# Three scheduling changes in a fused attention and gMLP kernel on one core: which units are scored by rows, when a modulation weight is used, and when the group loads are issued

## Chip, cores and metric

One core of one Trainium2 chip. The metric is the device time of the whole program in microseconds (us); the profile's span, from the first to the last instruction, is about 1.9 us shorter.

The engines are called as the profile calls them: PE (TensorE, matmuls), ACT (ScalarE), DVE (VectorE), POOL (GpSimd, which also issues DMAs), SP (SyncE, which issues the DMA transposes).

## The reference

Grouped-query attention, modulated by a condition vector `c`, followed by a gated MLP. Sizes: 2048 queries and keys, model width 512, 32 query heads in 8 groups, head width 128, MLP width 1792.

```python
mod = silu(c) @ w_mod                       # six rows of 512: sa, ca, ga, sb, cb, gb
h = layernorm(x) * (1 + ca) + sa
q = (h @ wq)                                # 32 heads of 128
p = softmax(q k^T / sqrt(128));  o = p v    # 4 heads share one group's k, v
x = x + ga * (o @ wo)
h = layernorm(x) * (1 + cb) + sb
z = gelu(h @ w_in); z1, z2 = halves of z; z2 = layernorm(z2)
x = x + gb * ((z1 * (w_sp @ z2 + b_sp)) @ w_out)
```

## The kernel before

The attention is a software pipeline over 128 *units*, a unit being one group (8) times 128 queries (16). Iteration `it` computes the scores of unit `it` in eight slots, and in the same slots the PV product of an earlier unit, the output projection of a still earlier one, and a piece of the next q. A unit's scores are made in one of two ways:

```python
    TURN_A, TURN_B = 3 * CT, (HKV - 1) * NT          # 12, 112
    def by_rows(u):
        return TURN_A <= u < TURN_B and u % 2 == 0
    def pv_at(u):
        return u + 3 if by_rows(u) else u + 1
```

- *Not by rows*: keys on the partitions. The exponentials land as PV needs them; PV is 64 matmuls of 129 columns (the last one sums the row), then DVE normalises and SP issues one small transpose, `oT<-onorm`.
- *By rows*: queries on the partitions. ACT accumulates the row sums, DVE normalises 128x2048 for each of four heads, and SP issues four transposes of 128x2048 into `pT`. PV is then 16 matmuls of 512 columns, two units later than otherwise, because the transposes need time.

The four buffers for a row unit's exponentials are slices of tiles that are idle during attention: three in the tile of `w_in`, one in `wmod_a`. Head 3's buffer is read by a transpose that the program places in slot 1 of the *next* unit, and it is needed again two units after its own.

```python
def turn_rows(u, hh):                       # DVE, then SP
    ...
    nc.vector.tensor_scalar(out=pn[hh], in0=pn[hh], scalar1=rinv, ...)
    nc.sync.dma_start_transpose(out=pTs[u][:, :, hh * P : (hh + 1) * P], in_=pn[hh])

def mod_rows():                             # ga and gb as rows on all partitions
    ...                                     # 32 one-column matmuls, two copies into modc
    for part, rows in ((2, ga_rows), (5, gb_rows)):
        line = dram.tile([D], FP32, ...)
        nc.gpsimd.dma_start(out=line[:].rearrange("(dt p) -> p dt", p=P), in_=modc[:, cols])
        nc.gpsimd.dma_start(out=rows[:], in_=line[:].partition_broadcast(P))
```

`mod_rows` therefore makes a chain of four DMAs on POOL: 2 KB out to DRAM, read back to all partitions, and once more. `at(it, slot, fn)` places a piece of work in *program order*. On PE and ACT, which are kept busy, that is also its time. On POOL, which has little to do, an instruction runs as soon as its buffer is free and the one before it is done, often many units earlier.

```python
    at(9, 4, mod_cols_b); at(10, 4, mod_rows)
    for g in range(1, HKV):
        it = (g - 1) * NT
        at(it + 7, 6, load_k(g))            # SP, a transpose out of DRAM
        at(it + 8, 3, load_v(g)); at(it + 9, 3, load_wo(g)); at(it + 7, 3, load_wq(g))   # POOL
```

## Time and profile before

| | before |
|---|---|
| device time, first three runs | 1316.68 us median, 1314.65 to 1318.89 |
| span of the profiled run | 1314.1 us |
| busy PE / ACT / DVE | 1305.1 / 1105.0 / 657.4 us |
| mean DMA rate | 119 GB/s, 156.79 MB |
| a pair of units, one by rows | 17.44 us |
| a pair of units, none by rows | 17.62 us |
| waits of PE in the waits view | 3.0 us |

The durations of a unit, here and below, are the distances between every eighth exponential of ACT in the timeline: unit *u* begins with exponential 8*u*. The waits view lists engine, line and tile, what it waited for, the total, the number and the longest.

### The profile page before, as it was taken

How to read it: one execution, taken by the hardware profiler on the slowest of the kernel's cores; microseconds unless marked ns; L12 is line 12 of the kernel's file. 1: busy time of each engine (PE TensorE's matmuls, PEld its weight loads, DVE VectorE, ACT ScalarE, POOL GpSimd, SP SyncE). 2: the span in 40 equal slices, each digit the busy share in tenths (PEclk: the TensorE clock that was granted, in tenths of full speed). 3: DMA queues.
4: the chain of work that ended last, by engine and by line, in shares of the span. 5: the costliest groups of instructions: out<-in, count | busy, mean ns of one | idle time of the engine just before them, and what ended most of it. 6: DMA issues, size and time to landing. Idle time of an engine off the chain costs nothing.

```text
span 1314.1 us, 25092 instructions
## 1 busy us (share of the span) xinstructions
PE 1305.1 (99%) x9959; PEld 755.5 (57%) x9959; DVE 657.4 (50%) x1612; ACT 1105.0 (84%) x1461; POOL 52.0 (4%) x96
## 2 busy tenths in 40 slices
PE   9999999999999999999999999999999999999998
PEld 5666555555555555555555555555556666644445
DVE  6624445444454544444455544444452566784444
ACT  7899999999999999999999999999998899650000
POOL 1101000000000000000000000000000000120000
PEclk9999999999999999999999999999999999999999
DMA  7554988878988888988897877688762232143200
GB/s 181 123 67 58 180 161 141 140 125 158 153 144 138 144 141 138 135 142 157 153 143 129 155 141 144 124 166 151 140 126 76 45 62 48 29 117 80 69 21 27
DMA packets 537741, 156.79 MB, mean 119 GB/s; under 512 B 527280, under 2 KB 533680, under 8 KB 537616
## 3 DMA queue, kind: packets, MB, share of 16 engines
q1 hardware_dynamic: 530592, 135.97, 60.3%
q0 software_dynamic: 4432, 16.91, 4.6%
q10 hardware_dynamic: 2592, 2.23, 0.5%
q8 instruction: 80, 1.31, 0.4%
q14 instruction: 45, 0.37, 0.1%
HBM read 21.89 MB, written 2.10 MB: 18 GB/s over the span
## 4 chain that ended last, share of the span: by engine, by line
PE 98%; DMA 1%; DVE 0%; issue 0%; ACT 0%; ACTq 0%; DVEq 0%
PE o_ps L1069 21%; PE s_ps L1013 20%; PE o_ps L1048 13%; PE s_ps L994 13%; PE misc L1101 8%; PE misc L944 8%; PE misc L1426 7%; PE s_ps L1260 2%; PE s_ps L1299 2%; PE o_ps L1447 1%; DMA pT<-wmod_a 1%; PE o_ps L785 1%; PE s_ps L1447 1%; PE misc L854 0%; PE o_ps L944 0%; DVE hT L813 0%
## 5 line engine op out<-in xcount | busy, mean ns | idle before, releaser
L1020 ACT ACTIVATE wsp<-s_ps 128x1024 bf16<-128x1024 f32 x408 | 416.2, 1025 | 19.5 <-PE s_ps L1013 3.5
L1013 PE MATMUL s_ps<-qT,kT 128*128 128x512 bf16 x1248 | 370.9, 379 | 1.9 <-ACT wmod_a L1001 1.6
L1001 ACT ACTIVATE win_sb<-s_ps 128x1024 bf16<-128x1024 f32 x300 | 307.0, 1025 | 6.2 <-ACT win_sb L1001 0.8
L1069 PEld LDWEIGHTS <-wsp 128*128 128x128 bf16 x3264 | 218.5, 98 | 96.3
L1069 PE MATMUL o_ps<-v,wsp 128*128 128x129 bf16 x3264 | 251.6, 220 | 0.0
L994 PE MATMUL s_ps<-kT,qT 128*128 128x512 bf16 x800 | 237.9, 379 | 0.0
L1048 PE MATMUL o_ps<-pT,v 128*128 128x512 bf16 x800 | 237.3, 379 | 0.0
L1020 ACT ACTIVATE pT<-s_ps 128x1024 bf16<-128x1024 f32 x216 | 217.3, 1026 | 20.6 <-PE s_ps L1013 8.3
L1101 PE MATMUL misc<-wo_g,oT 128*128 128x512 bf16 x512 | 194.0, 379 | 0.0
L1013 PEld LDWEIGHTS <-kT 128*128 128x128 bf16 x1248 | 121.0, 98 | 117.0 <-issue 4.4
L944 PE MATMUL misc<-hT,wq_g 128*128 128x512 bf16 (+2 forms) x520 | 187.0, 371 | 0.1
L1069 PEld LDWEIGHTS <-pT 128*128 128x128 bf16 x1728 | 115.3, 98 | 49.6
L955 DVE CAST qT<-misc 128x512 bf16<-128x512 f32 x125 | 85.5, 684 | 112.2 <-PE misc L944 112.2
L1048 PEld LDWEIGHTS <-v 128*128 128x128 bf16 x800 | 78.2, 98 | 94.4
L1069 PE MATMUL o_ps<-v,pT 128*128 128x129 bf16 x1728 | 132.5, 220 | 0.0
L1057 DVE CAST oT<-o_ps 128x512 bf16<-128x512 f32 x50 | 34.6, 691 | 173.7 <-PE o_ps L1048 173.7
L1035 DVE TENSOR_SCALAR win_sb<-win_sb,rall 128x2048 bf16<-128x2048 bf16 x150 | 113.0, 753 | 5.7 <-DVE rall L1034 0.5
L994 PEld LDWEIGHTS <-qT 128*128 128x128 bf16 x800 | 78.2, 98 | 52.5 <-issue 0.2
L1001 ACT ACTIVATE wmod_a<-s_ps 128x1024 bf16<-128x1024 f32 x100 | 102.4, 1024 | 2.3 <-DMA pT<-wmod_a 2.3
L1426 PE MATMUL misc<-wsp,z 128*128 128x512 bf16 (+2 forms) x560 | 100.7, 336 | 0.0
L1080 DVE RECIPROCAL rall<-o_ps 128x2 f32<-128x2 f32 x156 | 26.6, 170 | 135.1 <-PE o_ps L1069 131.4
L1031 DVE TENSOR_TENSOR tot<-rs 128x1 f32<-128x1 f32 x200 | 30.7, 154 | 120.6 <-ACT win_sb L1001 119.1
(106 smaller groups left out, 856.5 us busy)
## 6 DMA issues: line engine op xcount, KB each, us to landing
wq_g<-in_A_wq_dram POOLq DMA_DIRECT2D x7, 512.0 KB, 5.5
v<-in_A_v_cache_dram POOLq DMA_DIRECT2D x7, 512.0 KB, 5.9
wo_g<-in_A_wo_dram POOLq DMA_DIRECT2D x7, 512.0 KB, 3.8
pT<-win_sb SPq DMA_TRANSPOSE x150, 4.9
wsp<-in_w_mod_dram POOLq DMA_DIRECT2D x1, 2048.0 KB, 10.4
out_dram<-yout ACTq DMA_DIRECT2D x16, 128.0 KB, 1.7
win_sb<-in_B_w_in_dram POOLq DMA_DIRECT2D x1, 1792.0 KB, 9.3
x_sb<-in_A_x_dram SPq DMA_DIRECT2D x3, 512.0 KB, 5.3
```

The lines of the kernel that those rows point to most:

```text
L944: nc.tensor.matmul(ps[0][:, o0 : o0 + n], lhsT=wqs[g][:, dt, hh * DH : (hh + 1) * DH], rhs=hTs[ch][:, dt, c0 : c0 + n], start=(dt == 0), s ...
L955: nc.vector.tensor_copy(out=dst, in_=src)
L994: nc.tensor.matmul(s_ps[:, c * 512 : (c + 1) * 512], lhsT=qTs[b][:, hh, jj * P : (jj + 1) * P], rhs=groups[g]["kT"][:, k0 : k0 + 512], sta ...
L1001: nc.scalar.activation(out=pn[hh][:, half * HK : (half + 1) * HK], in_=s_ps[:], func=ACT.Exp, scale=inv_sqrt_dh, accum_out=rsums[u][:, i : ...
L1013: nc.tensor.matmul(s_ps[:, h * 512 : (h + 1) * 512].rearrange("p (r q) -> p r q", r=REP), lhsT=groups[g]["kT"][:, kt * P : (kt + 1) * P], ...
L1020: nc.scalar.activation(out=pTs[u][:, 2 * i : 2 * i + 2, :], in_=s_ps[:].rearrange("p (k q) -> p k q", k=2), func=ACT.Exp, scale=inv_sqrt_dh,)
L1035: nc.vector.tensor_scalar(out=pn[hh], in0=pn[hh], scalar1=rinv, scalar2=None, op0=ALU.mult)
L1048: nc.tensor.matmul(o_pss[u][:], lhsT=groups[g]["v1"][:, kt, 0:DH], rhs=pTs[u][:, kt, :], start=(kt == 0), stop=(kt == NKT - 1),)
L1057: nc.vector.tensor_copy(out=oTs[u][:], in_=o_pss[u][:].rearrange("p (r q) -> p r q", r=REP))
L1069: nc.tensor.matmul(o_ps[:, hh % 2, 0 : DH + 1], lhsT=pTs[u][:, kt, hh * P : (hh + 1) * P], rhs=groups[g]["v1"][:, kt, 0 : DH + 1], start=( ...
L1101: nc.tensor.matmul(X_ps[:], lhsT=oTs[u][:, hh, :], rhs=groups[g]["wo"][:, hh, :], start=(hh == 0), stop=(hh == REP - 1),)
L1426: nc.tensor.matmul(g_ps[:, :n], lhsT=z2[:, st, f * P : (f + 1) * P], rhs=wsp[t][:, st, c0 : c0 + n], start=(st == 0), stop=(st == NT - 1 a ...
```

## The change

The intent is to take more of PE's work in the cheaper, wide form: by rows from unit 8 on and not 12, and three units (112, 116, 120) of the last group too. For that the `wsp` buffer and the weights in it must be free earlier (the second part of `w_mod` is used in iterations 4 and 5, not 9 and 10), PV of the late row units comes five units later so that each fills an iteration that would have none, and the group loads are spread, one per pair of units.

```diff
-    TURN_A, TURN_B = 3 * CT, (HKV - 1) * NT
+    TURN_A, TURN_B = 2 * CT, (HKV - 1) * NT
     def by_rows(u):
-        return TURN_A <= u < TURN_B and u % 2 == 0
+        return u % 2 == 0 if TURN_A <= u < TURN_B else u % 4 == 0 and TURN_B <= u < NU - CT
     def pv_at(u):
-        return u + 3 if by_rows(u) else u + 1
+        return u + 1 if not by_rows(u) else u + 3 if u < TURN_B else u + 5
+    # three buffers (pT0, pT1, wsp), each unit takes the one that is free first
...
-    at(TURN_B + 3, 5, lambda: nc.gpsimd.dma_start(out=win_sb, in_=win_dram))
-    at(9, 4, mod_cols_b)
-    at(10, 4, mod_rows)
+    at(NU - CT - 1, 2, lambda: nc.gpsimd.dma_start(out=win_sb, in_=win_dram))
+    at(4, 4, mod_cols_b)
+    at(5, 4, mod_rows)
...
-    at(TURN_B + 4, 0, wsp0)
+    at(NU + 1, 0, wsp0)                      # and its 16 loads with it
...
-        at(it + 7, 6, lambda g=g: load_k(g))
-        at(it + 8, 3, lambda g=g: load_v(g))
-        at(it + 9, 3, lambda g=g: load_wo(g, nc.gpsimd))
-        at(it + 7, 3, lambda g=g: load_wq(g, nc.gpsimd))
+        at(it + 7, 4, lambda g=g: load_wq(g, nc.gpsimd))
+        at(it + 9, 5, lambda g=g: load_k(g))
+        at(it + 11, 4, lambda g=g: load_v(g))
+        at(it + 13, 4, lambda g=g: load_wo(g, nc.gpsimd))
```

More of the change, by code (lines that the diff above doesn't have):

```diff
@@ L962 @@
     NU = HKV * NT
-    TURN_A, TURN_B = 3 * CT, (HKV - 1) * NT
+    TURN_A, TURN_B = 2 * CT, (HKV - 1) * NT
     def by_rows(u):
-        return TURN_A <= u < TURN_B and u % 2 == 0
+        return u % 2 == 0 if TURN_A <= u < TURN_B else u % 4 == 0 and TURN_B <= u < NU - CT
     def pv_at(u):
-        return u + 3 if by_rows(u) else u + 1
+        return u + 1 if not by_rows(u) else u + 3 if u < TURN_B else u + 5
+    users, homes = dict(pT0=-2, pT1=-1, wsp=CT + 2), {}
+    for u in range(NU):
+        homes[u] = min(users, key=lambda k: users[k])
+        assert users[homes[u]] < u
+        users[homes[u]] = pv_at(u)
     rsums, pTs, onorms, oTs, xaccs, o_pss, h2Ts = {}, {}, {}, {}, {}, {}, {}
@@ L982, in qk @@
         if i == 0:
-            if TURN_A <= u <= TURN_B + 1 and u % 2 == 1:
+            if homes[u] == "wsp":
                 pTs[u] = wspp.tile([P, NT, 512], BF16, name="wsp")
             else:
-                pTs[u] = late.tile([P, NKT, 512], BF16, name="pT")
+                pTs[u] = late.tile([P, NKT, 512], BF16, name=homes[u], bufs=1)
             if by_rows(u):
@@ L1230, in set_fill @@
             if hole:
-                it, slot = hole, k // 2
+                it, slot = divmod(hole * NSLOT + k // 2 - 1, NSLOT)
             if b == 1:
@@ L1239, in wsp0 @@
         wsp[0] = wspp.tile([P, NT, 512], BF16, name="wsp")
-    at(TURN_B + 4, 0, wsp0)
+    at(NU + 1, 0, wsp0)
     for st in range(NT):
-        at(TURN_B + 4 + st // 2, 2 + 4 * (st % 2), lambda st=st: load_wsp(wsp[0], 0, st))
+        at(NU + 1 + st // 4, 2 * (st % 4), lambda st=st: load_wsp(wsp[0], 0, st))
     for g in range(1, HKV):
         it = (g - 1) * NT
-        at(it + 7, 6, lambda g=g: load_k(g))
-        at(it + 8, 3, lambda g=g: load_v(g))
-        at(it + 9, 3, lambda g=g: load_wo(g, nc.gpsimd))
-        at(it + 7, 3, lambda g=g: load_wq(g, nc.gpsimd))
+        at(it + 7, 4, lambda g=g: load_wq(g, nc.gpsimd))
+        at(it + 9, 5, lambda g=g: load_k(g))
+        at(it + 11, 4, lambda g=g: load_v(g))
+        at(it + 13, 4, lambda g=g: load_wo(g, nc.gpsimd))
     zs = {}
@@ L1350 @@
             zs["z2"] = z2p.tile([P, NT, FH], BF16, name="z2")
-        pvs = [u for u in (it - 3, it - 1) if 0 <= u < NU and pv_at(u) == it]
-        wos = [u for u in (it - 5, it - 3) if 0 <= u < NU and pv_at(u) + 2 == it]
+        pvs = [u for u in (it - 5, it - 3, it - 1) if 0 <= u < NU and pv_at(u) == it]
+        wos = [u for u in (it - 7, it - 5, it - 3) if 0 <= u < NU and pv_at(u) + 2 == it]
         wf = [fn for u in wos for fn in wo_proj(u)]
```

## The prediction

> **What bounds the kernel now.** I read the page first: busy time, the 40 slices and the chain that ended last.
>
> ```profile
> PE 1305.1 (99%) x9959; PEld 755.5 (57%) x9959; DVE 657.4 (50%) x1612; ACT 1105.0 (84%) x1461; POOL 52.0 (4%) x96
> ...
> PEclk9999999999999999999999999999999999999999
> ...
> PE 98%; DMA 1%; DVE 0%; issue 0%; ACT 0%; ACTq 0%; DVEq 0%
> ```
>
> TensorE (PE) works in 99% of the span at full clock, and the chain is 98% PE. So a change gains only what it takes off PE, or what it takes out of a stall of PE. The waits view then says how much of the second kind there is: of PE 3.0 us in all (three waits), but a stalled matmul counts as running, so I looked at ScalarE (ACT) too, whose exponentials free the score banks.
>
> The program has 128 units (a group of keys times 128 queries), each with eight exponentials of 128x1024, so every eighth exponential of ACT starts a unit. In every one of the 128 iterations PE does a unit's scores (16 matmuls of 512 columns), the PV product of an earlier unit, up to four matmuls of the output projection and up to four of the next q. Fifty units (even ones, 12 to 110) are "by rows": scores with queries on the partitions, transposed by DMA, PV as 16 matmuls of 512 columns at L1048. The other 78 do PV as 64 matmuls of 129 columns at L1069. The timeline of PE shows one slot (an eighth of an iteration) of either kind, first with the narrow PV, then with the wide one:
>
> ```profile
> 202.50 0.59 PE L994 MATMUL s_ps<-kT,qT 128*128 128x512 bf16 x2
> 202.93 0.62 PE L1069 MATMUL o_ps<-v,wsp 128*128 128x129 bf16 x8
> 203.39 0.38 PE L944 MATMUL misc<-hT,wq_g 128*128 128x512 bf16 x1
> 203.60 0.59 PE L994 MATMUL s_ps<-kT,qT 128*128 128x512 bf16 x2
> ...
> 210.21 0.59 PE L1013 MATMUL s_ps<-qT,kT 128*128 128x512 bf16 x2
> 210.64 0.59 PE L1048 MATMUL o_ps<-pT,v 128*128 128x512 bf16 x2
> 211.07 0.38 PE L944 MATMUL misc<-hT,wq_g 128*128 128x512 bf16 x1
> 211.29 0.59 PE L1013 MATMUL s_ps<-qT,kT 128*128 128x512 bf16 x2
> ```
>
> Start to start counts here, not the durations, which overlap. Eight narrow PV matmuls take 203.39 - 202.93 = 0.455 us, two wide ones 211.07 - 210.64 = 0.43 us; the slots last 1.10 and 1.08 us. So an iteration lasts 8 x 1.10 = 8.81 us with a narrow PV and 8 x 1.08 = 8.64 with a wide one. The timeline of ACT agrees: two units with rows between them start
>
> ```profile
> 193.46 8.52 ACT L1020 ACTIVATE wsp<-s_ps 128x1024 bf16<-128x1024 f32 x8
> 210.90 8.52 ACT L1020 ACTIVATE wsp<-s_ps 128x1024 bf16<-128x1024 f32 x8
> ```
>
> 17.44 us apart. In the last group, where no unit is by rows, unit follows unit in 8.81, a pair in 17.62. **A unit by rows is worth 0.18 us**, about 1% of a pair, and no more. (Bare ACT needs less: it makes eight exponentials by rows in 8.0 us where PE is ahead, at 118 to 126 us.)
>
> Last I looked for real stalls. ACT has one of size:
>
> ```profile
> 539.88 0.19 ACT L1001 ACTIVATION_READ_ACCUMULATOR win_sb<-s_ps 128x1 f32 x1
> 542.18 1.02 ACT L1001 ACTIVATE wmod_a<-s_ps 128x1024 bf16<-128x1024 f32 x1 [2.11 <-DMA pT<-wmod_a]
> ...
> DMA to landing us min/median/max: 4.2/4.3/13.3
> ```
>
> The last line is of the transposes out of wmod_a. One of 50 took 13.3 us instead of 4.3; it was issued at 528.82, and a load of wq_g issued at 528.90 took 12.2 us itself, against 4.6 to 4.8 in two other groups. ACT then waited for its buffer, and unit 60 lasted 10.75 us instead of 8.82.
>
> **What the Trainium skill says.** "TensorE: Matmul & The Clock Gate", section "Wait — 56ns, not 53.3ns?", gives start to start at full clock as the columns over 2.4 GHz plus about 2.5 ns: 55.6 ns for 128, 215.7 for 512. The trace agrees: 0.455 us / 8 = 57 ns for 129 columns, 0.43 / 2 = 216 ns for 512. So 64 narrow matmuls are 3.62 us and 16 wide ones 3.46: the wide form saves the fixed cost and the 129th column, nothing else. "DMA: Bandwidth & Descriptors", section "Issuing engines are not separate DMA queues", says that transfers from all issuing engines run on the same 16 DMA engines and interleave; the collision at 528.8 us, where both transfers were slow, agrees.
>
> **The change part by part.**
>
> By rows from 8, and 112, 116, 120: five more units (8 and 10 early, three late), so 55. PE loses 5 x 48 = 240 matmuls and 5 x 0.18 = **0.9 us**. ACT gets 40 accumulator reads, and DMA 20 transposes of 4.3 to 4.4 us less five small ones, all beside PE.
>
> PV five units later in the last group: deferral only. The old order ended its rows with two PVs in iteration 113 (unit 113 lasted 12.20 us = 8.81 plus one PV of about 3.4, nothing lost) and two output projections in iteration 115 (9.99 us against 8.81 plus 4 x 0.216 = 9.67: 0.3 us lost). Now 112 follows at 117, 116 at 121, 120 at 125, each into an iteration without another PV but the last. Two PVs meet in 125 (about 8.0 + 3.46 us) and two projections in 127, where there is no q projection. I count **0.3 us** gained, perhaps 0.
>
> The hole: the first deferred PV leaves an iteration short, at 13 before, at 9 now, filled with the same 16 q projections. Units 12 to 15 took 31.73 us; their PE work is about 30.6 (7.94, 7.78, 7.94, 6.91 from 0.216 and 0.057 us each), as ACT limits two of them. The same loss of about a microsecond moves to 8 to 11. Only the wait of 0.24 us for a transpose at 140 us may go, as the w_mod rows' small DMAs no longer run there: **0.2 us**.
>
> Second part of w_mod early: its 64 one-column matmuls (0.8 us in each of iterations 9 and 10, which lasted 9.61 instead of 8.81) move to 4 and 5, at the same cost. The load is at the same place; it was issued at 37.1 and landed at 47.5 us. Iteration 4 begins at 46.0 (ACT) and its slot 4 is at 50.0, so 2.5 us are to spare. VectorE and GpSimd work moves along, off the path.
>
> Group loads: wq, v and wo keep their order on GpSimd, which runs ahead and waits for a free buffer (wq_g waits 323 us in total), so their times hardly move; only k, on SP's queue, starts two units later. **0.**
>
> win_sb later (unit 123) and spatial weights wsp[0] at iteration 129: win_sb needs 9.3 us and is first read at 1130.7, some 40 us later. The 16 transposes of wsp[0] are issued at about 1.3 us each, 21 us from 1139 on; their use begins at 1184.9. The next 32 loads may start at 1166 instead of 1160, for use from 1209 on. **0.**
>
> Sum: 0.9 + 0.3 + 0.2 = 1.4 us less: 1316.68 - 1.4, rounded to **1315.3 us**.
>
> **The rivals.** (a) *DMA becomes the bound.* The DMA share is 0.8 to 0.9 in the row phase and 0.16 to 0.33 in the last group; four extra transposes every four units fit there, and a row unit at 8 starts only after the hT transposes (landed at 76.4). Against it: in 50 row units one transpose in the waits of ACT cost 2.1 us. It would cost some 2 to 4 us by chance, more if a PV waited for its transposes, which have over a unit to spare. (b) *The tail slips.* SP issues in order, and the xnT transposes of the last tiles now queue among wsp[0]'s loads. VectorE is nearly full there (14.5 of 16 us from 1139 to 1155), and the last z2 normalisation ends at 1183.9, some 4 us before PE reads those tiles. A slip of over 4 us would lengthen the span one for one; I estimate 1 to 2 at most, so hidden. (c) *The early move stalls PE:* wmod_b landing later than iteration 4's slot 4 costs its lateness, 2 to 5 us. Against it: nothing before its load changes. For a gain instead: v and wo of the next group now queue on GpSimd behind the mod rows, so that they no longer share DMA with the hT transposes at 60 to 76 us (8.5 to 13.7 us to landing); but PE did not wait there. (d) *The collisions vanish* with the k load moved: 2 us less. For it only that unit 60 was such a case; against it, that the transfer there was wq_g, whose time stays.
>
> **Range and chances.** The three runs of before spread over 4.2 us, 0.3%, about three times the gain I expect. With the chance stalls of (a) and (d) on either side: 1312.0 to 1318.5. Two per cent is 26 us; no part of the working comes near it. Faster by over 2%: 0.01; within: 0.97; slower: 0.02, for a PE or DMA stall that repeats in each group.
>
> **What would show it.** In the changed trace: 880 wide and 4672 narrow PV matmuls (before 800 and 4992), PE still 98% of the chain, row pairs at 17.44 us, units of the last group at 8.64 where 112 and 116 have their PV, 8.81 elsewhere; no unit of 12.20 at 113 but one near 11.5 at 125; units 4 and 5 longer by 0.8, 9 and 10 not. Wrong would be: PE waiting at L854 for wmod_b, PV waiting for a pT transpose in the last group, a gap before the first spatial matmul, or row pairs of another length. Then the step "DMA fits beside PE" fails, and the time leaves the range upwards.

## The result, and the profile after

| | before | after |
|---|---|---|
| median, same chip | 1315.66 us (4 runs, 1313.84 to 1318.89) | 1315.51 us (4 runs, 1315.24 to 1316.04) |
| ratio after / before | | 0.9997, 95% interval 0.9975 to 1.0018 |
| span of the profiled run | 1314.13 us | 1313.84 us |

A ratio is the mean time of one kernel's fast runs over that of the other's of the same rounds, so not quite the ratio of the medians. The times are the same within the noise, and the predicted 1315.3 us lies 0.2 us off. The two spans, cut at the same units, say that this agreement hides errors that cancel:

| stretch (units) | before | after | difference | predicted |
|---|---|---|---|---|
| start, 0 to 3 | 45.98 | 46.12 | +0.14 | 0 |
| 4 to 15 | 103.79 | 106.16 | **+2.37** | -0.6 |
| 16 to 111 | 838.85 | 837.12 | **-1.73** | 0 |
| 112 to 127 | 142.22 | 141.23 | -0.99 | -0.84 |
| after the last exponential | 183.30 | 183.21 | -0.09 | 0 |

(Predicted: two early row units and the wait at unit 14 make -0.36 - 0.24; three late ones and the pair of projections -0.54 - 0.3.)

First what stayed as it was. The busy times and the chain of the changed kernel, from its page:

```profile
PE 1294.6 (99%) x9545; PEld 744.9 (57%) x9719; DVE 675.8 (51%) x1657; ACT 1109.2 (84%) x1501; POOL 52.9 (4%) x96
...
PE 97%; DMA 1%; issue 1%; DVE 0%; SPq 0%; ACT 0%
```

PE is still 97% of the chain. The weight loads count the matmuls of the two forms better than the matmul records, of which some are missing; from the groups by line and form:

```profile
L1076 PEld LDWEIGHTS <-pT 128*128 128x128 bf16 x4544 | 303.8, 98 | 133.2
L1055 PEld LDWEIGHTS <-v 128*128 128x128 bf16 x880 | 86.1, 98 | 103.8
...
L1076 PEld LDWEIGHTS <-wsp 128*128 128x128 bf16 x128 | 8.6, 98 | 3.3
```

The reader sees 880 wide PV matmuls and 4544 + 128 = 4672 narrow ones, as predicted. The row pairs last 17.44 us, iterations 113, 117 and 121 of the last group 8.57 (their neighbours 8.82 to 8.87), 125 11.40. Units 4 and 5 are longer by 0.8 us each, as predicted.

The -1.73 us is the wait in unit 60 of the kernel before (10.75 us), which this trace of the changed one doesn't have. The +2.37 us is new. It sits in unit 10, which lasts 10.87 us; PE's waits show its first part:

```profile
PE misc L1108 <- DMA oT<-onorm: 1.2, 1, 1.2
PE s_ps L1020 <- ACT wmod_a L1008: 0.9, 1, 0.9
```

Before, the second of these two lines read 1.6 us (in unit 60) and the first did not exist. In the timeline of PE they are these instructions:

```profile
102.90 0.62 PE L1076 MATMUL o_ps<-v,pT 128*128 128x129 bf16 x8
104.69 0.39 PE L1108 MATMUL misc<-wo_g,oT 128*128 128x512 bf16 x1 [1.17 <-DMA oT<-onorm]
...
108.00 0.38 PE L1108 MATMUL misc<-wo_g,oT 128*128 128x512 bf16 x1
109.33 0.59 PE L1020 MATMUL s_ps<-qT,kT 128*128 128x512 bf16 x2 [0.95 <-ACT wmod_a L1008]
```

The output projection of unit 7 waits for its `oT`. That transpose is small and lands 2.6 us after its issue in the median of this trace (2.4 at the least). SP's timeline shows why it was late:

```profile
82.96 1.19 SPq L1096 DMA_TRANSPOSE oT<-onorm  x1
86.28 12.86 SPq L1045 DMA_TRANSPOSE wsp<-win_sb  x3
99.30 1.20 SPq L1096 DMA_TRANSPOSE oT<-onorm  x1
100.60 3.75 SPq L1045 DMA_TRANSPOSE wsp<-wmod_a  x1
104.41 2.86 SPq L743 DMA_TRANSPOSE kT<-in_A_k_cache_dram  x1
```

The second column is the time that SP takes to *issue*, as the profile records it. Three of unit 8's transposes occupied SP for 12.86 us, the first alone for 7.9, and the `oT` of unit 7 stood behind them in the same queue. It was issued at 99.30 and landed at 104.64. What slowed them is in the timeline of POOL:

```profile
60.91 0.83 POOL L1180 DMA_DIRECT2D mod<-modc  x1 [0.85 <-DVE modc L1178]
70.44 0.57 POOL L1181 DMA_DIRECT2D ga_rows<-mod  x1 [8.71 <-DMA mod<-modc]
71.00 0.76 POOL L1180 DMA_DIRECT2D mod<-modc  x1
81.05 0.55 POOL L1181 DMA_DIRECT2D gb_rows<-mod  x1 [9.29 <-DMA mod<-modc]
81.59 0.76 POOL L720 DMA_DIRECT2D wq_g<-in_A_wq_dram  x1
...
82.48 1.17 POOL L728 DMA_DIRECT2D v<-in_A_v_cache_dram  x1
83.63 0.77 POOL L738 DMA_DIRECT2D wo_g<-in_A_wo_dram  x1
```

Before, POOL issued these three loads of group 1 (1.5 MB) at 59 to 61 us:

```profile
59.11 0.82 POOL L720 DMA_DIRECT2D wq_g<-in_A_wq_dram  x1
...
60.11 1.31 POOL L728 DMA_DIRECT2D v<-in_A_v_cache_dram  x1
61.41 0.76 POOL L738 DMA_DIRECT2D wo_g<-in_A_wo_dram  x1
```

Now the chain of `mod_rows` stands ahead of them, each copy to DRAM takes over 9 us, and the loads start at 81.6 to 83.6, just ahead of the first transposes of unit 8 at 86.3. That is the theory for the experiments: **theory 1, the held-up loads meet unit 8's transposes**. Its rivals: the short iterations around the first deferred PV cost this wherever they stand; the load of k, now in SP's queue at 104 us, is to blame; or it is chance, as in unit 60.

### The profile page after: what moved, and what is told of

Its sections match the earlier page's. It is cut to its first block, busy times and chain, and to the rows that moved or that the text cites. A ratio compares the mean times of both kernels' runs of the same rounds, so it can differ in the third digit from the quotient of the medians.

```text
span 1313.8 us, 24616 instructions
## 1 busy us (share of the span) xinstructions
PE 1294.6 (99%) x9545; PEld 744.9 (57%) x9719; DVE 675.8 (51%) x1657; ACT 1109.2 (84%) x1501; POOL 52.9 (4%) x96
## 4 chain that ended last, share of the span: by engine, by line
PE 97%; DMA 1%; issue 1%; DVE 0%; SPq 0%; ACT 0%
PE o_ps L1076 20%; PE s_ps L1020 20%; PE s_ps L1001 15%; PE o_ps L1055 14%; PE misc L1108 8%; PE misc L944 8%; PE misc L1433 7%; PE s_ps L1267 2%; PE s_ps L1306 2%; PE o_ps L1454 1%; PE s_ps L1454 0%; DMA kT<-in_A_k_cache_dram 0%; DMA oT<-onorm 0%; PE o_ps L944 0%; PE misc L854 0%
## 5 line engine op out<-in xcount | busy, mean ns | idle before, releaser
L1027 ACT ACTIVATE pT<-s_ps 128x1024 bf16<-128x1024 f32 x568 | 576.6, 1024 | 34.0 <-PE s_ps L1020 9.5
L1076 PEld LDWEIGHTS <-pT 128*128 128x128 bf16 x4544 | 303.8, 98 | 133.2
L1076 PE MATMUL o_ps<-v,pT 128*128 128x129 bf16 x4544 | 349.8, 220 | 1.2
L1020 PE MATMUL s_ps<-qT,kT 128*128 128x512 bf16 x1168 | 347.4, 379 | 2.8 <-ACT wmod_a L1008 0.9
L1008 ACT ACTIVATE win_sb<-s_ps 128x1024 bf16<-128x1024 f32 x330 | 337.5, 1024 | 7.2 <-PE s_ps L1001 1.2
L1001 PE MATMUL s_ps<-kT,qT 128*128 128x512 bf16 x857 | 257.0, 379 | 2.9
L1055 PE MATMUL o_ps<-wsp,v 128*128 128x512 bf16 x426 | 128.1, 379 | 0.6
L1055 PE MATMUL o_ps<-pT,v 128*128 128x512 bf16 x410 | 123.8, 380 | 0.6
L1433 PEld LDWEIGHTS <-z 128*128 128x128 bf16 x560 | 50.6, 98 | 48.5
L1121 DVE TENSOR_TENSOR xacc<-misc,xacc 128x512 f32<-128x512 f32 x112 | 76.2, 680 | 0.0
```

The costliest lines, as they stand in the source:

```text
L1001: nc.tensor.matmul(s_ps[:, c * 512 : (c + 1) * 512], lhsT=qTs[b][:, hh, jj * P : (jj + 1) * P], rhs=groups[g]["kT"][:, k0 : k0 + 512], sta ...
L1008: nc.scalar.activation(out=pn[hh][:, half * HK : (half + 1) * HK], in_=s_ps[:], func=ACT.Exp, scale=inv_sqrt_dh, accum_out=rsums[u][:, i : ...
L1020: nc.tensor.matmul(s_ps[:, h * 512 : (h + 1) * 512].rearrange("p (r q) -> p r q", r=REP), lhsT=groups[g]["kT"][:, kt * P : (kt + 1) * P], ...
L1027: nc.scalar.activation(out=pTs[u][:, 2 * i : 2 * i + 2, :], in_=s_ps[:].rearrange("p (k q) -> p k q", k=2), func=ACT.Exp, scale=inv_sqrt_dh,)
L1055: nc.tensor.matmul(o_pss[u][:], lhsT=groups[g]["v1"][:, kt, 0:DH], rhs=pTs[u][:, kt, :], start=(kt == 0), stop=(kt == NKT - 1),)
L1076: nc.tensor.matmul(o_ps[:, hh % 2, 0 : DH + 1], lhsT=pTs[u][:, kt, hh * P : (hh + 1) * P], rhs=groups[g]["v1"][:, kt, 0 : DH + 1], start=( ...
```

## The experiments

Twelve kernels ran; all gave correct results. Kernels are compared only within the same rounds. The stretches are from one trace of each, in us. No kernel differs by 2% from the kernel before; the intervals that exclude 1 are those of e1 and e3 (faster) and of e6 and e4 (slower).

| run | median (runs) | before | ratio (95%) | units 4-7 | 8-11 | 12-15 | 16-111 | 112-127 |
|---|---|---|---|---|---|---|---|---|
| changed, again | 1316.74 (6) | 1319.01 (11) | 0.9988 (0.9966, 1.0009) | 36.79 | 34.03 | 34.88 | 837.12 | 141.23 |
| e1 | 1314.20 (6) | 1319.01 | 0.9967 (0.9946, 0.9989) | 38.95 | 31.90 | 34.88 | 837.12 | 141.23 |
| e3 | 1314.01 (6) | 1319.01 | 0.9963 (0.9942, 0.9984) | 36.79 | 35.23 | 31.90 | 838.96 | 141.18 |
| e6 | 1328.17 (6) | 1319.01 | 1.0070 (1.0039, 1.0100) | 36.79 | 43.39 | 34.88 | 837.12 | 141.23 |
| e8 | 1316.84 (6) | 1317.04 (11) | 0.9993 (0.9975, 1.0011) | 36.79 | 31.91 | 34.88 | 841.37 | 141.23 |
| e9 | 1320.09 (6) | 1317.04 | 1.0012 (0.9995, 1.0030) | 36.79 | 31.90 | 34.88 | 844.00 | 141.23 |
| e4 | 1320.91 (4) | 1317.04 | 1.0025 (1.0003, 1.0046) | 36.79 | 35.29 | 35.23 | 845.46 | 137.54 |
| e2 | 1315.67 (4) | 1317.04 | 0.9986 (0.9965, 1.0007) | 36.85 | 35.17 | 31.63 | 837.07 | 142.23 |
| e10 | 1313.84 (5) | 1315.61 (9) | 0.9988 (0.9974, 1.0001) | 36.79 | 31.90 | 34.88 | 837.12 | 141.98 |
| e12 | 1313.77 (5) | 1315.61 | 0.9987 (0.9973, 1.0001) | 35.28 | 36.77 | 31.63 | 837.07 | 142.24 |
| e7 | 1316.38 (1) | | | 36.79 | 34.28 | 34.88 | 837.07 | 142.24 |
| e5 | 1320.91 (1) | | | 36.79 | 34.31 | 34.88 | 838.65 | 145.40 |

**The changed kernel again.** No edit.

> The changed kernel once more, unaltered, for its spread and to see whether the wait in unit 10 belongs to the kernel or to chance. Theory 1 (the loads of group 1, held up on GpSimd behind the w_mod rows, meet the transposes of unit 8): the wait recurs, unit 10 lasts 10.4 to 11.2 us, units 8 to 11 together 34 to 35 us, time 1315.2 to 1316.2 us. Theory 2 (chance, like the wait of the kernel before in unit 60): unit 10 lasts about 8.4 us, units 8 to 11 about 32 us, and the time falls to about 1313.3 us.

Units 8 to 11 took 34.03 us: the wait recurs, so it belongs to the kernel. (34.28 in e7 and 34.31 in e5, which leave this part alone, 34.49 in the first trace.) The times spread over 1315.0 to 1318.6, wider than expected, and the median is 1 us higher than in the first call; the kernel before ran up to 1323.3 here.

**e1: the loads of group 1 ahead of the w_mod rows.**

```diff
+        if g == 1:
+            at(5, 3, lambda: load_wq(1, nc.gpsimd))
+            at(5, 3, lambda: load_v(1))
+            at(5, 3, lambda: load_wo(1, nc.gpsimd))
+            at(it + 9, 5, lambda: load_k(1))
+            continue
```

> The changed kernel with one edit: wq, v and wo of group 1 are issued just ahead of the w_mod rows (iteration 5, slot 3), so that they start at about 60 us and not at 82 to 84. Theory 1 (these loads slow unit 8's transposes, SP's queue holds up the oT transpose of unit 7, and PE waits for it in iteration 10): no wait in unit 10, units 8 to 11 together 31.7 to 32.3 us instead of 34.5, time 2.2 to 2.8 us below the changed kernel, 1312.7 to 1313.3. Rival (the short iterations around the first deferred PV cost this wherever they stand): units 8 to 11 stay at 34 to 35 us and the time at 1315.5. A loss elsewhere is possible: the hT transposes of 61 to 76 us then share DMA with 1.5 MB again.

Units 8 to 11 fell to 31.90 us, so theory 1 holds for unit 10. But most of the gain reappeared in unit 7, 10.77 us instead of 8.75, by the same kind of wait:

```profile
80.70 0.39 PE L1108 MATMUL misc<-wo_g,oT 128*128 128x512 bf16 x1 [1.85 <-DMA oT<-onorm]
```

The loads, the small DMAs and the hT transposes now all ran at 60 to 81 us, and another `oT` took 13.1 us to land. In the trace the net gain over the repeat of the changed kernel is zero (spans 1313.16 and 1313.14); in the timed runs the median fell by 2.5 us, as expected (to 1314.20, not to 1313, as the changed kernel itself was slower), but with no gain in the trace that fall is not explained: it may be chance waits in the runs that left no trace. The prediction of the loss elsewhere was right, its size was not foreseen.

**e3: rows from unit 12 again.**

```diff
-    TURN_A, TURN_B = 2 * CT, (HKV - 1) * NT
+    TURN_A, TURN_B = 3 * CT, (HKV - 1) * NT
```

> The changed kernel with rows from unit 12 on again (TURN_A = 3 * CT), all else as changed. Theory 1: the loads at 82 to 94 us now meet no row transposes, no wait over 0.5 us in units 8 to 15; two row units fewer cost 0.36 us, the wait of 2.5 us goes: 1313.2 to 1314.0 us. Rival (the hole itself costs the 2.5 us): the wait moves to unit 14, units 12 to 15 last 34 to 35 us instead of 31.7, time 1315.5 to 1316.2 us.

Units 12 to 15 took 31.90 us and none waited. So the first deferred PV doesn't cost the 2 us by itself: the early row units cost it, because of what they meet. By the medians of the same rounds, the changed kernel is 2.7 us better *without* its early row units (1314.01 against 1316.74; 1313.19 to 1315.35 against 1315.02 to 1318.59); in the traces units 4 to 15 are 1.8 us shorter (103.92 against 105.70), so part of the 2.7 is not located. Unit 60 waited in this trace as in the kernel before (10.81 us), with the same pair of slow transfers; that question returns below.

**e6: the old places of the group loads.**

```diff
-        at(it + 9, 5, lambda g=g: load_k(g))
+        at(it + 7, 6, lambda g=g: load_k(g))
```

(and v, wo, wq in program order as before)

> The changed kernel with the loads of wq, k, v and wo at the places of the kernel before. Theory 1 (GpSimd runs ahead, only k moves): wq, v and wo are issued within 0.5 us of where they were, k of the later groups two units earlier; the wait in unit 10 stays or grows by up to 1 us as k of group 1 joins the others; 1315.2 to 1316.5 us. Rival (k of group 1 in SP's queue at 104 us is what holds up the row transposes): the wait shrinks by 1 us or more, 1313.5 to 1314.5 us.

Theory 1 and the rival both failed on size: units 8 to 11 took 43.39 us, 9.4 us more than in the repeat. In the steady state, 16 to 111, nothing changed at all. So the spread of the loads is worth nothing for groups 2 to 7 and 9 us in this one place. What differs there: k's 512 KB were issued at 75.19 us and took 14.1 us to land, the second small copy to DRAM 12 us and more, and wq, v and wo came at 84.8 to 87.3 us, 3 us later than in the changed kernel, where theory 1 had said 0.5. That k sets this off is argued; the run moves all four loads, and no run moves k alone. The timelines of SP and ACT show the wait:

```profile
86.09 23.61 SPq L1045 DMA_TRANSPOSE wsp<-win_sb  x3
```

```profile
105.61 1.02 ACT L1008 ACTIVATE win_sb<-s_ps 128x1024 bf16<-128x1024 f32 x1 [6.37 <-DMA wsp<-win_sb]
```

Three issues took 23.6 us instead of 12.9, and ACT waited 6.37 us for the first row buffer to be read out. PE waited 6.4 us for ACT, and here a wait cost more than itself: in the view by stretches the clock granted to PE is 1.00 up to 103 us, 0.73 from 103 to 104, 0.50 from 104 to 110 and 1.00 again from 111. After the pause narrow matmuls followed each other in 108 ns and not in 57, up to 110.1 us, which is some 1.6 us of the 9.4 (an estimate from these spacings). The mean clock of e6's runs, 0.993 to 0.998, is the lowest of all kernels.

**e8: the small DMAs of the w_mod rows later.** The matmuls stay in iteration 5; only the four DMAs move.

```diff
+    def mod_lines():                        # the two pairs of DMAs, taken out of mod_rows
     at(5, 4, mod_rows)
+    at(28, 0, mod_lines)
```

> The changed kernel with one edit: the four small DMAs of the w_mod rows are issued at iteration 28 (their matmuls stay in iteration 5), so that GpSimd isn't held up and issues wq, v and wo of group 1 at about 60 us as the kernel before does. Theory 1 (unit 10 waits because these loads come at 82 to 84 us): units 8 to 11 about 31.9 us, unit 7 about 8.8 us and not the 10.8 of the run with the loads first, as the small DMAs are gone there too; 2.2 to 2.8 us below the changed kernel, span about 1311. Rival (the small DMAs of the w_mod rows are harmless and unit 7's wait comes of the loads at 60 us alone): unit 7 lasts 10 to 11 us again, only 0.3 to 0.6 us below the changed kernel.

In units 4 to 15 everything came as theory 1 says: unit 7 8.75, unit 10 8.26, units 8 to 11 31.91 us. The loads still ran at 60 us beside the hT transposes, so e1's wait in unit 7 needs the small DMAs. SP's issue of unit 8's three transposes took 7.62 us:

```profile
86.21 7.62 SPq L1045 DMA_TRANSPOSE wsp<-win_sb  x3
93.99 1.19 SPq L1096 DMA_TRANSPOSE oT<-onorm  x1
```

But the sum didn't fall: units 16 to 111 took 4.25 us more. POOL reached the moved DMAs at 167 us, and unit 20 lasted 11.24 us; unit 28 lasted 10.96, by a meeting of `wq_g` and a transpose out of `wmod_a` (13.2 and 13.5 us to landing). Compare SP at this place with the next run, in which the small DMAs are not there yet while the load of `v` is in both (e8 first):

```profile
170.55 11.82 SPq L1045 DMA_TRANSPOSE pT<-win_sb  x3
```

```profile
170.40 8.04 SPq L1045 DMA_TRANSPOSE pT<-win_sb  x3
```

The load of v, 512 KB, took 9.38 us beside the small DMAs and 5.10 without; in the DMA views of the two runs, with the time to landing last:

```profile
v<-in_A_v_cache_dram POOLq DMA_DIRECT2D x1, 512.0 KB, 9.4
```

```profile
v<-in_A_v_cache_dram POOLq DMA_DIRECT2D x1, 512.0 KB, 5.1
```

**Theory 1 is incomplete: the 2 KB DMAs alone are enough to slow the others.**

**e9: as e8, and wq after v and wo.**

```diff
-        at(it + 7, 4, lambda g=g: load_wq(g, nc.gpsimd))
         at(it + 9, 5, lambda g=g: load_k(g))
         at(it + 11, 4, lambda g=g: load_v(g))
-        at(it + 13, 4, lambda g=g: load_wo(g, nc.gpsimd))
+        at(it + 11, 5, lambda g=g: load_wo(g, nc.gpsimd))
+        at(it + 11, 6, lambda g=g: load_wq(g, nc.gpsimd))
```

> As e8, and wq of each group is issued after its v and wo, which takes it from slot 3 of an odd unit (when the fourth transpose of a unit by rows is issued) to slot 7. Theory (the chance waits of 1 to 2 us and the spread between runs come of wq meeting the transpose out of wmod_a): no transpose out of wmod_a over 7 us in the trace, no unit from 16 to 111 over 9.0 us, spread of the runs under 2 us, median up to 1 us below e8. Rival (chance waits have another cause): spread and median as e8, long transposes stay.

A miss in time, and a half-hit in the trace. From unit 32 on no transpose out of `wmod_a` took over 7 us. But the small DMAs now met wq and row transposes at 185 to 215 us, and unit 22 lasted 15.85 us (the granted clock was 0.66 from 210 to 215 us, after PE had paused for 3.9 us). The runs fall in two clusters, 1317.6 to 1318.0 and 1320.1 to 1320.5.

**e4: no unit by rows.**

```diff
     def by_rows(u):
-        return u % 2 == 0 if TURN_A <= u < TURN_B else u % 4 == 0 and TURN_B <= u < NU - CT
+        return False
```

(and the q projections spread evenly)

> The changed kernel with no unit by rows at all, q projections spread evenly. It measures what a unit by rows is worth. If 0.18 us each: every unit from 16 to 123 lasts 8.81 us; 55 x 0.18 = 9.7 us are lost, the wait in unit 10 (2.2) and the short iterations (about 1.2) are gained, span 1319.0 to 1320.5, some 6 to 7 us above the changed kernel's 1313.1 to 1313.8. If PE's narrow PV were worth a different amount, e.g. 0.3 us, span over 1325. With hardly any large transposes the spread of the runs should fall under 1 us if DMA collisions make it.

Sixteen units took 140.91 us instead of 139.52: (140.91 - 139.52) / 8 = 0.174 us for each of the eight row units in them, against 0.18 predicted. The span was 1319.05 us. The four runs lie within 0.15 us, 1320.84 to 1320.99: without the large transposes the run-to-run spread is gone.

**e2: in the kernel before, only the second part of w_mod early.**

```diff
-    at(9, 4, mod_cols_b)
-    at(10, 4, mod_rows)
+    at(4, 4, mod_cols_b)
+    at(5, 4, mod_rows)
```

> The kernel before with only the second part of w_mod early (matmuls in iterations 4 and 5, not 9 and 10). Theory: the cost moves, it doesn't change: units 4 and 5 longer by 0.8 us each, 9 and 10 shorter by 0.8 each, the wait of 0.24 us at unit 14 gone, units 0 to 15 together 138.0 to 138.6 us (138.5 before), and wq, v and wo of group 1 issued at 82 to 86 us without harm, as no unit by rows runs then. Rival (the early move itself makes PE wait): units 4 to 8 over 37.5 us.

Units 0 to 15 took 138.40 us (138.54 before), as expected: the early move alone is free, since no row unit runs near its DMAs. It is harmful only together with row units from 8 on.

**e10: as e9, with the small DMAs in the last group**, issued from ACT's queue in iterations 113 and 114.

> As e9 (wq after v and wo), with the four small DMAs of the w_mod rows issued in the last group (iterations 113 and 114, from ScalarE's queue), where DMA is at 0.16 to 0.33 and few transposes run. Theory 3 (the small DMAs of the w_mod rows slow everything that shares DMA with them, wherever they stand; wq in slot 7 meets nothing): units 8 to 11 at 31.9 us, every pair from 12 to 111 at 17.44, no wait over 0.5 us in units 4 to 123, span 1310.6 to 1311.4, median 1312.4 to 1313.2 us, spread under 2 us; about 3 us below the changed kernel. Rival (wq after wo is what made e9 slow at unit 22, with 15.85 us): unit 22 again over 12 us.

Units 4 to 111 are free of waits: 31.90 us for 8 to 11, 17.44 for every pair after. Unit 22 is 8.82 us, so its wait in e9 came of the small DMAs and not of wq's place. The span, 1312.2, is 1 us longer than expected: 0.75 of it is in units 113 and 114, where two of unit 112's transposes took 13.35 and 10.99 us to land beside the small DMAs. My expectation missed that they slow the few transposes there too. The median, 1313.84 us, is above the 1312.4 to 1313.2 expected as well; the runs lie within 1.0 us.

**e12: the kernel before with wq after v and wo**, otherwise unaltered.

> The kernel before with wq of each group issued after its v and wo, nothing else. If the kernel's chance waits (unit 60: 10.75 us) and its spread (1314 to 1323 us) come of wq meeting the transpose out of wmod_a: no such transpose over 7 us from 150 us on, no unit from 16 to 111 over 9.0 us, median 1313.5 to 1315 us, spread under 2.5 us. Rival (another cause): median and spread as the kernel before, 1316 to 1319 and 6 to 9 us.

The wait in unit 60 is gone. The view of the tile `wmod_a` gives the time to landing of its transposes:

```profile
DMA to landing us min/median/max: 4.2/4.3/5.8
```

The longest was 13.3 us before. The five runs lie within 0.3 us (1313.54 to 1313.84), while the kernel before in the same rounds ran from 1313.65 to 1317.26. So this one order of three loads is the source of its spread. By the medians it is worth 1.8 us; the interval of the ratio (0.9973 to 1.0001) just includes 1. That the wait in unit 60 is gone from one trace would by itself show little, since e2's trace, with wq at its old place, has none either.

**e7: no row units in the last group.**

```diff
-        ... else u % 4 == 0 and TURN_B <= u < NU - CT
+        ... else False
```

> The changed kernel without the three units by rows in the last group. Theory (0.18 us each and 0.3 to 0.4 us for the pair of output projections in one iteration): units 112 to 127 together 142.1 to 142.3 us, as the kernel before has them (142.2), against 141.23. Rival (late rows are worth nothing because ACT or DMA binds there): 141.2.

Units 112 to 127 took 142.24 us, as the kernel before. The late row units and the even spread of PV are worth 1.01 us.

**e5: PV of the late row units three units later, not five.**

```diff
-        return u + 1 if not by_rows(u) else u + 3 if u < TURN_B else u + 5
+        return u + 1 if not by_rows(u) else u + 3
```

> The changed kernel with PV of the last group's units by rows three units later, as everywhere else, not five. By rows only every fourth unit, PV at 115, 119 and 123 then meets another PV, and iterations 117 and 121 have none. Theory: an iteration without PV holds 5.2 us of PE work and ACT needs 7.4, so each loses about 2.2 us and units 112 to 127 take 145 to 146.5 us instead of 141.23. Rival (deferral is free in whatever order): 141.2 to 141.6.

145.40 us, 4.2 more than with five. Iterations 117 and 121, without PV, lasted 8.23 us though they hold 5.2 us of PE work, and 115, 119 and 123 with two PVs 12.20, 11.34 and 11.34. Five is better because it makes each row unit's PV fall into the next one's empty iteration. (Its 838.65 us in 16 to 111 is a wait in unit 28, 10.50 us, where a transpose out of `wmod_a` took 13.1 us to land.)

## Why the prediction was right or wrong

**Right: PE bounds, and 0.18 us a row unit.** e4 measured 0.174. Everything large in the prediction rests on this, and it held. (The prediction's 3.62 and 3.46 us for the PV of a unit, estimates that it doesn't call so, are slightly off; the last section has the sum.)

**Right: the last group.** The late row units and the projections were put at 0.84 us together; e7 measured 1.01, and the profile pair 0.99. "Deferral only" was right for the distance chosen; e5 shows that it is not right in general.

**Right: the tail, and the early move itself.** The span after the last exponential changed by -0.09 us although 16 transposes were moved into it, and e2 shows the move of w_mod to be free alone. PE's waits list none for `wmod_b`.

**Wrong: "VectorE and GpSimd work moves along, off the path."** This is the step that failed, and with it "the same loss of about a microsecond moves to 8 to 11" and the 0.2 us gained there. The prediction saw that v and wo would queue on GpSimd behind the w_mod rows, and counted it as a possible gain for the hT transposes. It did not follow the queue one step further, to where the loads end up: at 82 to 94 us, on unit 8's transposes. Units 4 to 15 cost 2.4 us more where 0.6 less was predicted. Even without the wait the 0.6 is not all there: in e8 and e10 these units took 103.57 us, 0.2 less than before. The loss that was to move is 0.27 us larger in the changed kernel (the four units around the first deferred PV took 31.90 us in e1, e3, e9 and e10, 31.63 in e2 and e12, which have the q projections of the kernel before); the change fills them in one slot earlier, and whether that is the reason was not tested. e2 (the early move harmless alone), e3 (no early row units, no wait) and e8 (no small DMAs there, loads early, no wait) show the cause to be the meeting.

**Wrong in reasoning, though not in the steady state: "Group loads: 0."** e6 shows zero for units 16 to 111 and 9.4 us for units 8 to 11. The spread of the loads keeps them out of a crowd that the change itself makes; which of the four loads matters most there is open.

**Not foreseen: a wait that fell by chance.** Rival (d), a wait less in unit 60, is what the profile pair shows, -1.73 us. It was named and given little weight, as wq's place stays, and that reason was right: e6, with k back at its old place, has no such wait in 16 to 111. It belongs to the meeting of wq and the transpose out of `wmod_a`, which both kernels can have; the changed one had a mild case in its first trace (10.6 and 10.2 us to landing at 252 us, no wait) and in its repeat (7.8 and 7.2 us at 391). e12 shows the cause. Why it hits unit 60 in one kernel's traces and nothing in another's is open.

So the closeness is luck: the time was predicted within 0.2 us because an unforeseen loss of 2.4 us in one place stood against a lost wait of 1.7 us in another. In the second round of timing both kernels were slower (0.9988, interval 0.9966 to 1.0009). Rid of their meetings, the two designs come out alike: e10 1313.84 us, e12 1313.77 in the same rounds. Both are below the medians of the kernel before in every call (1315.61 to 1319.01), and of the changed one in both calls; the interval of their ratios to the kernel before just includes 1. An untried combination, e12 with the late row units, would by the 1.01 us of e7 come to about 1312.8 us: an estimate from these two runs.

## What to carry to other kernels

A DMA that is hidden where it stands is not free to move: follow it, and all that queues behind it on its issuing engine, to what runs at the new time. When a kernel's runs spread while another form of it is steady to 0.15 us, look for two transfers that are issued at the same moment (528.82 and 528.90 us here), and reorder one of them. A wait of PE can also cost more than its length, when the granted clock falls in it, as in e6. And when a total comes out as predicted, compare the stretches before believing the reasons.

## What the Trainium skill lacked or had wrong

- "DMA: Bandwidth & Descriptors", section "Issuing engines are not separate DMA queues", calls the sequencer's time to start a DMA "usually small relative to the DMA itself". Here SP's issue of a 128x2048 transpose took 1.3 to 3.2 us of 4.2 to 5.4 in nine of ten cases from 260 to 980 us of the changed kernel, 7.9 of 9.9 us in the crowd at 86 us, and 15.5 of 20.4 us in e6. As SP issues in order, that time was what delayed the small `oT` transposes and stalled PE. With the rest of the section, that transfers of all engines run on the same 16 DMA engines and interleave, these runs agree: two issued by SP and POOL at 528.82 and 528.90 us took 13.3 and 12.2 us to land.
- The same page, section "Latency and other measured facts", gives a floor of about 0.8 us for tiny transfers, but no time for one in four-byte elements. The copy of 2.0 KB from 128 partitions to DRAM took 8.6 to 14.2 us to land (9.8 in a stretch where the DMA share was 0.20), and transfers beside it were slow: a load of 512 KB took 9.4 instead of 5.1 us, an `oT` transpose issued 3 us after it landed with it (80.94 and 80.77 us), 6.8 us after its issue and not 2.4. Why it holds up the others is not shown by these runs.
- "TensorE: Matmul & The Clock Gate", section "Wait — 56ns, not 53.3ns?": nothing to mend. From its rule, columns over 2.4 GHz plus 2.5 ns, follow 3.60 us for 64 matmuls of 129 columns and 3.45 for 16 of 512: 0.15 us less, an estimate, where e4 measured 0.174.
